# Second MLP of an attention-and-two-MLPs kernel: two weight-quadrant buffers, single transfers for a unit's weights, units split two ahead, four end buffers

## The chip, the cores and the metric

The kernel runs on one core of a Trainium2 chip. The metric is the time of one execution in microseconds of device time; where several executions are given, their median counts. All inputs and outputs are float32 in the core's HBM.

## The reference, cut to what matters

```python
def reference(**kwargs):
    attn_out = _attn_ref(...)              # windowed and global attention, 4 x 8 heads
    x = attn_out as (2304, 512)
    x = _moe_ref(x, w_gate, w_val, w_out, rms_g)   # first MLP, 512 -> 1536 -> 512
    return _moe2_ref(x, w_in, w_out)               # second MLP

def _moe2_ref(x, w_in, w_out):             # 2304 x 512, 512 x 2048, 2048 x 512
    h = x @ w_in
    g = np.maximum(0.01 * h, h)
    return (g @ w_out).astype(np.float32)
```

The change concerns the second MLP and the last stores of the first.

## The kernel before, in words

Every float32 matrix product is made of three passes: an operand is split into a high part (a cast on ScalarE, `high`) and a low part (a subtraction on VectorE, `low`), and `mm3` issues high x high, low x high and high x low. Attention and the first MLP run first, software-pipelined; at the end of each block of columns of the first MLP `out_half` copies the four accumulators `yp` to `ys` tiles (ScalarE and VectorE in turn, two buffers of tag `sq`) and stores them to `y_dram` in HBM. Meanwhile the weights of the second MLP are narrowed to float32 and stored to HBM as `w2_f32[f][0]` (first layer) and `w2_f32[f][1]` (second layer), f from 0 to 15. All of this is ordered by a planner that simulates the program.

The second MLP splits the 2,304 columns into a rest of 128 and two halves (s = 0, 1) of 1,024. For each half eight up steps (`up`, one for each pair j of weight chunks) and then eight down steps (`dn`) run. An up step makes the products of a 2 x 2 block scheme with seven products in place of eight (products 1, 6, 7, 5, 2, 4, 3, six matmuls of 512 columns each, in the banks px, pw, py, pz); VectorE adds the banks up (x1, u2, v, h), ScalarE applies the leaky function. A down step multiplies the hidden columns (split into `d`) with w_out and keeps eight accumulators `o`; the last down step of a half copies them to `ob` tiles, which use the places of x1, u2 and v, and stores them.

In the first half the weights of pair j are loaded as quadrants into the tile q (`load_q`, 512 KB in two transfers), summed on VectorE (`weight_sums`), split in two parts (`make_w` with place 0, 1 and 2, each called inside the up step of the pair before) and stored for the second half (`keep_parts`, 1.8 MB, transfer `w_dram<-wr`). The tile q has one buffer, and `load_q(j + 1)` follows `keep_parts(j)`. Pair 0 was prepared during the first MLP, and `load_q(1)` stands ahead of the hand-ordered part, where the planner places it.

The rest of 128 columns is computed in 32 small units, three matmuls each (bank pr in the first layer, po in the second), two to an up step: `rest_run` runs one at each of two places. A unit's 256 KB of weights are loaded by `rest_load` into one of two `raw` buffers (four transfers of 64 KB in the first layer), split by `rest_split` into an `rw` tile, and used by `rest_step`, which then splits the weights of the next unit and loads those of the third. `rest_first`, called in the first up step, loads the rest's 128 columns (transfer `yr<-y_dram`), splits them and unit 0. `rest_turn` transposes four hidden chunks (bank pt) into `hid`; every fourth unit of the second layer splits four of them into `hr`. Six `dop` buffers are shared by `rw` and `d`.

From the second MLP on, the order on TensorE, VectorE, ScalarE and SP is that of the program, written out by hand (`manual_schedule`); each engine runs its queue in order, and SP issues all the transfers. A tile of the second MLP's memory pool lies where tiles of the first MLP's pool lay, and its first use waits for those alone; tiles are laid out in the order of their first use.

Of the kernel before, what the change touches and what calls it, by code (L numbers as in the profile page):

```python
# [24 lines left out]
def tile_window_global_attention_two_mlps(  # L25
# [38 lines left out]
    w2_f32 = [[dram.tile([P, DM], F32, name=f"w2_f32{k}_{f}") for k in range(2)] for f in range(NF2)]  # L64
# [528 lines left out]
    def out_half(g, hs, m0):  # L593
        i, f = step_of(g)
        n = BLOCKS1[i]
        for m in range(m0, m0 + KC // 2):
            if f == 0:
                yp[i, m] = pools[0].tile([P, 512], F32, tag="y", bufs=4, name=f"yp{i}_{m}")
            mm3(yp[i, m][:, 0:n], [w[:, m * P:(m + 1) * P] for w in wsp[g, 2]], hs, f == 0, f == NF1 - 1)
        flush()  # L600
        if f == NF1 - 1:
            for m in range(m0, m0 + KC // 2):
                ys = mp.tile([P, NX], F32, tag="sq", bufs=2, name=f"ys{i}_{m}")
                if m % 2:
                    nc.vector.tensor_copy(ys[:, 0:n], yp[i, m][:, 0:n])
                else:
                    nc.scalar.copy(ys[:, 0:n], yp[i, m][:, 0:n])
                nc.sync.dma_start(out=y_dram[:, m, cols[i]:cols[i] + n], in_=ys[:, 0:n])
# [297 lines left out]
    def load_q(j):  # L906

        if j < PAIRS:
            q = wq[j] = quarter()
            for s, f in ((0, j + PAIRS), (2, j)):  # L910
                nc.sync.dma_start(out=q[:, s:s + 2].rearrange("p s c -> p (s c)"), in_=w2_f32[f][0])
# [16 lines left out]
    def make_w(g, place):  # L928
# [9 lines left out]
        elif s == 0:  # L938
# [5 lines left out]
            elif place == 1:  # L944
                low(wq["parts"][0][1], q[:, wq["parts"][0][2]], wq["parts"][0][0])
                high(wq["parts"][1][0], q[:, wq["parts"][1][2]])
            else:
                low(wq["parts"][1][1], q[:, wq["parts"][1][2]], wq["parts"][1][0])
                keep_parts(j)
                load_q(j + 1)  # L950
# [26 lines left out]
    def rest_load(u):  # L977
# [4 lines left out]
        if u < NRU:  # L982
            fq, kc = divmod(u, KC)
            for x in range(4):
                nc.sync.dma_start(out=raw[:, x * P:(x + 1) * P], in_=w2_f32[4 * fq + x][0][:, kc * P:(kc + 1) * P])
        else:
            nc.sync.dma_start(out=raw, in_=w2_f32[u - NRU][1])

    def rest_split(u):

        if u >= NRU + NF2:
            return
        t = rest["w", u] = halves_tile(f"rw{u}")
        split(t[:, 0], t[:, 1], rest.pop(("raw", u)))
        if u >= NRU and u % 4 == 0:
# [3 lines left out]
    def rest_first():  # L999
        y = wp2.tile([P, HALF], F32, tag="x1", name="yr32")  # L1000
        nc.sync.dma_start(out=y.rearrange("p (k c) -> p k c", k=KC), in_=y_dram[:, :, 0:REST])
        rest["y"] = wp2.tile([P, 2, KC, P], F32R, tag="yr", name="yr")
        split(rest["y"][:, 0].rearrange("p k c -> p (k c)"), rest["y"][:, 1].rearrange("p k c -> p (k c)"), y)
        rest["hid"] = wp2.tile([P, NF2, P], F32, tag="hid", name="hid")
        rest_split(0)
        rest_load(2)
# [7 lines left out]
    def rest_step(u):  # L1014
# [22 lines left out]
        if u + 1 != NRU:  # L1037
            rest_next(u)

    def rest_next(u):  # L1040
        rest_split(u + 1)
        rest_load(u + 3)

    units = [lambda u=u: rest_step(u) for u in range(NRU + NF2)]

    def rest_run(s, j, place):

        total = (s * PAIRS + j) * 2 + place + 1
        while units and NRU + NF2 - len(units) < total:
            units.pop(0)()  # L1050

    def hidden(s, j):
        return hid[s, j]
# [12 lines left out]
    def up(g):  # L1066
# [12 lines left out]
        if j == 0:  # L1079
            rest_first() if s == 0 else rest_next(NRU - 1)  # L1080
# [12 lines left out]
        make_w(g + 1, 2)  # L1093
        rest_run(s, j, 1)
# [12 lines left out]
    def dn(g):  # L1107
# [21 lines left out]
        else:  # L1129
            for x in (2, 3):  # L1130
                dop_of(s, 4 * j + x)
            make_w(g + 1, 0)
# [12 lines left out]
    load_q(1)  # L1145
    with tc.manual_schedule(engines={mybir.EngineType.PE, mybir.EngineType.DVE, mybir.EngineType.Activation,
                                     mybir.EngineType.SP}):
        rest_load(0)
# [62 lines left out]
```

## Time and profile before

| | us |
|---|---|
| three runs | 990.54, 992.22, 992.23 |
| median | 992.22 |
| the profiled execution | 993.27 |
| its span, first to last instruction | 991.5 |
| TensorE busy in the span | 938.8 (95%) |
| VectorE busy | 586.2 (59%) |
| ScalarE busy | 459.2 (46%) |
| mean granted TensorE clock | 0.981 |

All times in the views below are microseconds from the start of the span. In the rows PE is TensorE, PEld its weight loads, DVE is VectorE, ACT is ScalarE, SPq is the queue of transfers that SP issues. A line number belongs to the kernel before and can be that of a helper: L77 is `mm3`, L81 `high`, L84 `low`, L985 the unit's load in `rest_load`. Buffer numbers are left out of the names. A matmul's duration in a row overlaps with those of its neighbours, since matmuls are pipelined; the pace is read from the stretch, not from the mean of one. The granted clock is a share of 2.4 GHz, and the lower of the two levels is 1.2 GHz.

The second MLP begins near 599.5: first up stage to 717.05, first down stage to 805.71, second up stage to 900.32, second down stage to the end.

### The profile page before, as it was taken

The page shows a single profiled execution, that of the slowest core. Times are in us where ns is not written, and L with a number is a line of the kernel's source. Part 1 is how long each engine was busy: PE and PEld are TensorE (multiplying, and loading weights), DVE is VectorE, ACT ScalarE, POOL GpSimd, SP SyncE. Part 2 cuts the span into 40 slices and gives each one's busy share as a digit, 9 for nine tenths or more (in the row PEclk, how much of TensorE's full clock was granted, in tenths as well). Part 3 has the DMA queues.
Part 4 walks back from the last instruction along what each step waited for, and adds up shares of the span by engine and source line. Part 5 has one row for each costly group of instructions (what it writes and reads, how often), then busy time and mean ns, then how long its engine had stood idle before and what let it go on. Part 6 is the DMA issues. An engine that isn't in the chain of part 4 may idle for free.

```text
span 991.5 us, 14141 instructions
## 1 busy us (share of the span) xinstructions
PE 938.8 (95%) x5056; PEld 760.8 (77%) x5056; DVE 586.2 (59%) x1216; ACT 459.2 (46%) x958; POOL 4.5 (0%) x26
## 2 busy tenths in 40 slices
PE   6799989999999999999999997899899989999998
PEld 4557667777777777778999995676688768888886
DVE  5689975596576876535677634556535624445332
ACT  6877665565454654424544322334343423334322
POOL 1000000000000000000000000000000000000000
PEclk9899999999999999999999998999999989999999
DMA  9497994786769999544999942665522265551113
GB/s 314 151 308 258 298 321 153 259 307 213 265 225 368 348 369 365 175 145 147 339 298 318 377 141 80 223 221 204 172 81 86 64 244 198 195 211 55 43 43 106
DMA packets 87942, 215.38 MB, mean 217 GB/s; under 512 B 12224, under 2 KB 26048, under 8 KB 85824
## 3 DMA queue, kind: packets, MB, share of 16 engines
q1 hardware_dynamic: 87872, 214.47, 62.9%
q8 instruction: 40, 0.66, 0.3%
q14 instruction: 30, 0.25, 0.1%
HBM read 154.14 MB, written 60.29 MB: 216 GB/s over the span
## 4 chain that ended last, share of the span: by engine, by line
PE 61%; DMA 12%; DVE 7%; ACT 3%; SPq 3%; issue 2%; DVEq 0%; ACTq 0%
PE o L77 12%; PE pg L77 11%; PE yp L77 10%; PE pv L77 10%; PE pz L77 3%; PE py L77 2%; PE px L77 2%; DMA q<-y_dram 2%; PE po L145 2%; DMA wr<-w_f 2%; PE sc L145 2%; DMA raw<-w_f 2%; DMA w<-w 2%; DMA q<-w_f 2%; PE pp L254 1%
## 5 line engine op out<-in xcount | busy, mean ns | idle before, releaser
L77 PE MATMUL o<-wr,d 128*128 128x512 f32 x768 | 175.4, 390 | 0.6 <-DVE wr L84 0.5
L77 PEld LDWEIGHTS o<-wr,d 128*128 128x128 f32 x768 | 143.9, 188 | 31.8 <-DVE wr L84 1.0
L77 PE MATMUL pg<-xh,w 128*128 128x512 f32 (+1 forms) x464 | 132.6, 367 | 0.4 <-ACT xh L81 0.4
L77 PE MATMUL pv<-xh,w 128*128 128x512 f32 (+1 forms) x464 | 129.5, 361 | 0.0
L77 PE MATMUL yp<-hsh,w 128*128 128x512 f32 (+1 forms) x480 | 123.8, 365 | 2.3 <-ACT hsh L81 1.7
L77 PEld LDWEIGHTS yp<-hsh,w 128*128 128x128 f32 x480 | 83.6, 188 | 16.0 <-ACT hsh L81 2.8
L77 PEld LDWEIGHTS pg<-xh,w 128*128 128x128 f32 x464 | 80.8, 188 | 17.6 <-issue 5.6
L77 PEld LDWEIGHTS pv<-xh,w 128*128 128x128 f32 x464 | 82.3, 188 | 11.4 <-issue 0.9
L77 PE MATMUL pg<-xl,w 128*128 128x512 f32 (+1 forms) x232 | 83.2, 359 | 0.0
L77 PE MATMUL pv<-xl,w 128*128 128x512 f32 (+1 forms) x232 | 83.1, 358 | 0.0
L81 ACT CAST w<-wf 128x512 fp32r<-128x512 f32 x92 | 56.5, 615 | 43.1 <-PE yp L77 23.5
L77 PE MATMUL yp<-hsl,w 128*128 128x512 f32 (+1 forms) x240 | 74.9, 362 | 0.2 <-DVE hsl L84 0.2
L234 ACT ACTIVATE s_ring<-s_ring,mx 128x224 f32<-128x224 f32 x128 | 60.2, 472 | 31.0 <-DVE mx L231 30.7
L84 DVE TENSOR_TENSOR w<-wf,w 128x512 fp32r<-128x512 f32 x92 | 62.9, 685 | 16.2 <-ACT w L81 15.4
L77 PE MATMUL pz<-ysb,wr 128*128 128x512 f32 x192 | 56.3, 434 | 0.6
L84 DVE TENSOR_TENSOR wr<-wr 128x1024 fp32r<-128x1024 f32 x16 | 19.6, 1224 | 62.6 <-ACT wr L81 62.4
L81 ACT CAST hsh<-th 128x512 fp32r<-128x512 f32 (+1 forms) x60 | 33.3, 556 | 49.2 <-DVE th L826 48.1
L826 DVE SCALAR_TENSOR_TENSOR th<-th,pv 128x512 f32<-128x512 f32 (+1 forms) x60 | 36.2, 603 | 29.9 <-PE pv L77 29.3
L84 DVE TENSOR_TENSOR d<-h,d 128x512 fp32r<-128x512 f32 x64 | 41.1, 685 | 13.8 <-ACT d L81 13.6
L77 PEld LDWEIGHTS yp<-hsl,w 128*128 128x128 f32 x240 | 43.7, 188 | 6.6 <-DVE hsl L84 0.5
L77 PEld LDWEIGHTS pg<-xl,w 128*128 128x128 f32 x232 | 43.5, 188 | 6.7 <-DVE xl L84 0.3
L81 ACT CAST wr<-wr 128x1024 fp32r<-128x1024 f32 x16 | 16.8, 1050 | 67.4 <-DMA wr<-w_f 67.4
(158 smaller groups left out, 1480.0 us busy)
## 6 DMA issues: line engine op xcount, KB each, us to landing
w<-w_dram SPq DMA_DIRECT2D x84, 512.0 KB, 5.8
w<-w SPq DMA_DIRECT2D x36, 512.0 KB, 5.8
w_dram<-w SPq DMA_DIRECT2D x36, 512.0 KB, 4.1
w64b<-w SPq DMA_DIRECT2D x32, 512.0 KB, 6.8
wf<-w_f SPq DMA_DIRECT2D x60, 256.0 KB, 4.4
w_dram<-wr SPq DMA_DIRECT2D x8, 1792.0 KB, 6.8
wr<-w_dram SPq DMA_DIRECT2D x8, 1792.0 KB, 8.1
kq<-kqv SPq DMA_DIRECT2D x32, 352.0 KB, 5.2
```

What stands on the lines that cost most here:

```text
L77: nc.tensor.matmul(dst, lhs[a], rhs[b], start=first and i == 0, stop=last and i == 2, skip_group_check=onto)
L81: nc.scalar.copy(hi, src)
L84: nc.vector.tensor_tensor(out=lo, in0=src, in1=hi.bitcast(F32), op=ALU.subtract)
L145: x = nc.tensor.matmul(dst, lhs, rhs, start=start, stop=stop)
L234: x = nc.scalar.activation(out=sp, in_=sp, func=AF.Exp, bias=mx[:, c:c + 1], scale=-1.0, accum_out=sm[:, c:c + 1])
L254: nc.tensor.transpose(pp[:, n * P:(n + 1) * P], s[:, c0:c0 + P], ident)
L826: nc.vector.scalar_tensor_tensor(out=t, in0=t, scalar=0.5, in1=pp[1][:, 0:n], op0=ALU.mult, op1=ALU.mult)
```

## The change

Six things are changed:

- `load_q`: pairs with an even number are loaded into a tile of tag `h7` (the place of the last pair's hidden tile), those with an odd number into q as before; `load_q(j + 2)` follows `keep_parts(j)`. `load_q(1)`, `load_q(2)` and the load of the rest's columns now stand at the head of the hand-ordered part.
- The first-layer weights lie in four HBM tiles of four row blocks each (`w2_fours`), so that a unit's weights are one transfer of 256 KB.
- `rest_split` stands two units ahead of the use, and a split is followed by the load for the unit two further on.
- `BESIDE` gives the number of units in each up step: none in the first of the first half, then 3, 3, 2, 2, 2, 2, 2; two in each of the second half.
- `rest_first` is cut in three: the load at the start, the splits of the columns and of units 0 and 1 at the end of the first up step (`rest_second`), and the splits of the first hidden columns and of units 16 and 17 in the last down step of the first half (`rest_third`).
- At the end of the first MLP's last block the four `ys` tiles are the four parts of one tile (`ys_end`, tag `xh`) instead of two buffers in turn.

```diff
@@ -61,7 +61,8 @@
     y_dram = dram.tile([P, KC, NTOK], F32, name="y_dram")
     w1_f32 = [[dram.tile([P, DM], F32, name=f"w1_f32{k}_{f}") for k in range(3)] for f in range(NF1)]
     HK = KC // 2 * P
-    w2_f32 = [[dram.tile([P, DM], F32, name=f"w2_f32{k}_{f}") for k in range(2)] for f in range(NF2)]
+    w2_fours = [dram.tile([P, 4, DM], F32, name=f"w2_fours{f}") for f in range(NF2 // 4)]
+    w2_f32 = [(w2_fours[f // 4][:, f % 4], dram.tile([P, DM], F32, name=f"w2_f32_{f}")) for f in range(NF2)]
     w2_dram = [dram.tile([P, 2, 7 * HK], F32, name=f"w2_dram{j}") for j in range(NF2 // 2)]
     w1_dram = [[dram.tile([P, 2, DM], F32, name=f"w1_dram{k}_{f}") for k in range(3)] for f in range(NF1)]
     ph1 = ctx.enter_context(ExitStack())
@@ -599,8 +600,10 @@
             mm3(yp[i, m][:, 0:n], [w[:, m * P:(m + 1) * P] for w in wsp[g, 2]], hs, f == 0, f == NF1 - 1)
         flush()
         if f == NF1 - 1:
+            if i == NI - 1 and m0 == 0:
+                yp["end"] = mp.tile([P, KC, NX], F32, tag="xh", bufs=2, name="ys_end")
             for m in range(m0, m0 + KC // 2):
-                ys = mp.tile([P, NX], F32, tag="sq", bufs=2, name=f"ys{i}_{m}")
+                ys = yp["end"][:, m] if i == NI - 1 else mp.tile([P, NX], F32, tag="sq", bufs=2, name=f"ys{i}_{m}")
                 if m % 2:
                     nc.vector.tensor_copy(ys[:, 0:n], yp[i, m][:, 0:n])
                 else:
@@ -906,7 +909,7 @@
     def load_q(j):
 
         if j < PAIRS:
-            q = wq[j] = quarter()
+            q = wq[j] = quarter() if j % 2 else wp2.tile([P, 8, HK], F32, tag=f"h{PAIRS - 1}", name=f"q{j}")
             for s, f in ((0, j + PAIRS), (2, j)):
                 nc.sync.dma_start(out=q[:, s:s + 2].rearrange("p s c -> p (s c)"), in_=w2_f32[f][0])
 
@@ -947,7 +950,7 @@
             else:
                 low(wq["parts"][1][1], q[:, wq["parts"][1][2]], wq["parts"][1][0])
                 keep_parts(j)
-                load_q(j + 1)
+                load_q(j + 2)
 
 
     PRODUCT = {1: (1, "a", 0), 6: (4, "a", 1), 7: (5, "a", 2),
@@ -981,29 +984,38 @@
         raw = rest["raw", u] = wp2.tile([P, HALF], F32, tag="raw", bufs=2, name=f"raw{u}")
         if u < NRU:
             fq, kc = divmod(u, KC)
-            for x in range(4):
-                nc.sync.dma_start(out=raw[:, x * P:(x + 1) * P], in_=w2_f32[4 * fq + x][0][:, kc * P:(kc + 1) * P])
+            nc.sync.dma_start(out=raw.rearrange("p (f c) -> p f c", c=P), in_=w2_fours[fq][:, :, kc * P:(kc + 1) * P])
         else:
             nc.sync.dma_start(out=raw, in_=w2_f32[u - NRU][1])
 
     def rest_split(u):
 
-        if u >= NRU + NF2:
-            return
-        t = rest["w", u] = halves_tile(f"rw{u}")
-        split(t[:, 0], t[:, 1], rest.pop(("raw", u)))
-        if u >= NRU and u % 4 == 0:
+        if u < NRU + NF2:
+            t = rest["w", u] = halves_tile(f"rw{u}")
+            split(t[:, 0], t[:, 1], rest.pop(("raw", u)))
+            rest_load(u + 2)
+
+    def rest_cols(u):
+
+        if NRU <= u < NRU + NF2 and u % 4 == 0:
             t = rest["h"] = wp2.tile([P, 2, 4, P], F32R, tag="yr", name=f"hr{u}")
             split(t[:, 0], t[:, 1], rest["hid"][:, u - NRU:u - NRU + 4])
 
     def rest_first():
-        y = wp2.tile([P, HALF], F32, tag="x1", name="yr32")
-        nc.sync.dma_start(out=y.rearrange("p (k c) -> p k c", k=KC), in_=y_dram[:, :, 0:REST])
+        rest["y32"] = wp2.tile([P, HALF], F32, tag="hn", name="yr32")
+        nc.sync.dma_start(out=rest["y32"].rearrange("p (k c) -> p k c", k=KC), in_=y_dram[:, :, 0:REST])
+
+    def rest_second():
         rest["y"] = wp2.tile([P, 2, KC, P], F32R, tag="yr", name="yr")
-        split(rest["y"][:, 0].rearrange("p k c -> p (k c)"), rest["y"][:, 1].rearrange("p k c -> p (k c)"), y)
+        split(*(rest["y"][:, h].rearrange("p k c -> p (k c)") for h in range(2)), rest["y32"])
         rest["hid"] = wp2.tile([P, NF2, P], F32, tag="hid", name="hid")
         rest_split(0)
-        rest_load(2)
+        rest_split(1)
+
+    def rest_third():
+        rest_cols(NRU)
+        rest_split(NRU)
+        rest_split(NRU + 1)
 
     def rest_turn(fq, hn):
         pt = lone(f"pt{fq}")
@@ -1034,23 +1046,20 @@
                 store_rows(0, ob)
         if turn:
             rest_turn(*turn)
-        if u + 1 != NRU:
-            rest_next(u)
-
-    def rest_next(u):
-        rest_split(u + 1)
-        rest_load(u + 3)
+        if u < NRU - 2 or u >= NRU:
+            rest_cols(u + 1)
+            rest_split(u + 2)
 
     units = [lambda u=u: rest_step(u) for u in range(NRU + NF2)]
 
+
+    BESIDE = {0: (0, 3, 3, 2, 2, 2, 2, 2), 1: (2,) * 8}
+
     def rest_run(s, j, place):
 
-        total = (s * PAIRS + j) * 2 + place + 1
-        while units and NRU + NF2 - len(units) < total:
+        n = BESIDE[s][j]
+        for _ in range(n // 2 if place else n - n // 2):
             units.pop(0)()
-
-    def hidden(s, j):
-        return hid[s, j]
 
 
     SLOTS = ((0, 0), (0, 1), (1, 0), (1, 1))
@@ -1076,8 +1085,6 @@
         product(s, j, 7, by)
         plus(v, u2, by)
         make_w(g + 1, 0)
-        if j == 0:
-            rest_first() if s == 0 else rest_next(NRU - 1)
         rest_run(s, j, 0)
         bz = bank(f"pz{s}_{j}")
         product(s, j, 5, bz)
@@ -1091,6 +1098,8 @@
         product(s, j, 4, by, False)
         plus(h[:, 1], u2, by)
         make_w(g + 1, 2)
+        if (s, j) == (0, 0):
+            rest_second()
         rest_run(s, j, 1)
         product(s, j, 3, bz, False)
         plus(h[:, 2], u2, bz)
@@ -1129,6 +1138,8 @@
         else:
             for x in (2, 3):
                 dop_of(s, 4 * j + x)
+            if s == 0:
+                rest_third()
             make_w(g + 1, 0)
             for n, t in enumerate(range(NT2 - 1, -1, -1) if s else range(NT2)):
                 for x in range(4):
@@ -1142,9 +1153,11 @@
                 k, d = divmod(j - 1, 2)
                 dn.columns = (s + 1, k, d * HK, columns_in(s + 1, k, d * HK))
 
-    load_q(1)
     with tc.manual_schedule(engines={mybir.EngineType.PE, mybir.EngineType.DVE, mybir.EngineType.Activation,
                                      mybir.EngineType.SP}):
+        load_q(1)
+        load_q(2)
+        rest_first()
         rest_load(0)
         rest_load(1)
         for g in range(NU):
```

## Rows read from the trace of the kernel before

**Rows 1.** Busy time by stage: stretch, length, each engine, granted clock, DMA share, GB/s.
```profile
599.46:717.05 117.59, 101.29 (x398) 76.54 (x397) 62.25 (x101) 45.78 (x66) 0.00 (x0) 0.93 0.56 189
805.71:824.16 18.45, 14.37 (x53) 11.19 (x52) 6.86 (x11) 5.00 (x9) 0.00 (x0) 0.81 0.56 199
824.16:889.44 65.28, 65.28 (x289) 54.07 (x288) 29.89 (x45) 23.37 (x33) 0.00 (x0) 1.00 0.61 218
```

**Rows 2.** The same table for three weight pairs of the first up stage.
```profile
632.36:648.34 15.98, 13.43 (x54) 10.13 (x52) 9.19 (x15) 5.75 (x8) 0.00 (x0) 0.92 0.56 189
648.34:660.73 12.39, 12.13 (x49) 9.14 (x48) 6.72 (x13) 5.85 (x8) 0.00 (x0) 0.97 0.66 224
703.66:717.05 13.39, 11.79 (x49) 8.90 (x48) 5.24 (x8) 5.55 (x8) 0.00 (x0) 1.00 0.61 217
```

**Rows 3.** Waits, first up stage: who <- for whom: total us, times, longest.
```profile
ACT wr L81 <- DMA q<-w_f: 31.4, 6, 5.8
...
PE pr L77 <- ACT rw L81: 14.1, 8, 5.5
```

**Rows 4.** Timeline, fourth pair: start, duration, engine, operation, count, [idle before <-releaser].
```profile
633.44 0.32 SPq L681 DMA_DIRECT2D w_dram<-wr  x1
...
633.81 1.37 SPq L911 DMA_DIRECT2D q<-w_f  x2
...
642.43 0.83 ACT L81 CAST wr<-q 128x768 fp32r<-128x768 f32 x1 [5.82 <-DMA q<-w_f]
...
644.32 1.22 PE L77 MATMUL pr<-rw,yr 128*128 128x512 f32 x3 [2.46 <-ACT rw L81]
...
645.64 2.90 PE L77 MATMUL pz<-ysb,wr 128*128 128x512 f32 x6
```

**Rows 5.** Timeline, start of the second MLP.
```profile
599.67 3.21 SPq L608 DMA_DIRECT2D y_dram<-ys  x4
...
602.59 1.66 PE L77 MATMUL pw<-ysa,wr 128*128 128x512 f32 x6 [1.59 <-DVE ys L605]
602.93 3.80 SPq L985 DMA_DIRECT2D raw<-w_f  x8
...
604.49 0.84 ACT L81 CAST wr<-q 128x768 fp32r<-128x768 f32 x1 [2.00 <-DMA y_dram<-ys]
...
606.84 0.58 SPq L1001 DMA_DIRECT2D yr<-y_dram  x1
609.97 0.62 ACT L81 CAST yr<-yr 128x512 fp32r<-128x512 f32 x1 [4.64 <-DMA yr<-y_dram]
...
611.16 1.22 PE L77 MATMUL pr<-rw,yr 128*128 128x512 f32 x2 [5.55 <-ACT rw L81]
```

**Rows 6.** DMA issues, first up stage: transfer, count, KB each, median us to landing.
```profile
w_dram<-wr SPq DMA_DIRECT2D x7, 1792.0 KB, 6.8
raw<-w_f SPq DMA_DIRECT2D x64, 64.0 KB, 2.0
...
y_dram<-ys SPq DMA_DIRECT2D x4, 160.0 KB, 1.8
```

**Rows 7.** Landing of the two raw loads issued from 621.7 to 623.0.
```profile
DMA to landing us min/median/max: 5.6/6.1/6.6
```

**Rows 8.** Timeline of SP's queue, planned stretch: load of quadrants 1.
```profile
554.43 1.60 SPq L911 DMA_DIRECT2D q<-w_f  x2
```

**Rows 9.** Planned stretch 425 to 550: store of a narrowed weight, and busy time.
```profile
w_f<-wfb SPq DMA_DIRECT2D x6, 256.0 KB, 4.4
...
425.00:550.00 125.00, 123.16 (x771) 112.67 (x771) 78.50 (x151) 54.63 (x105) 0.00 (x0) 1.00 0.77 256
```

**Rows 10.** Timeline, turn from the first half to the second.
```profile
810.87 0.58 ACT L1073 COPY x<-px 128x512 f32<-128x512 f32 x1 [2.15 <-DMA out<-ob]
...
811.81 0.69 DVE L964 TENSOR_TENSOR u<-x,pw 128x512 f32<-128x512 f32 x1 [2.29 <-DMA out<-ob]
...
812.54 0.50 PE L77 MATMUL po<-rw,hr 128*128 128x512 f32 x1 [2.59 <-ACT hr L81]
```

## The prediction

> **What bounds the kernel now.** I read the stage table first [rows 1]. The first up stage of the second MLP (eight weight pairs on the first 1,024 columns, from the first px product to the first o product) lasts 117.59 us, with TensorE busy for 101.29 at a granted clock of 0.93. The second up stage does the same products: six of its pairs take 65.28 us, all busy at clock 1.00, so 10.88 us a pair of 48 matmuls, 0.2267 us each. The first up stage has 384 matmuls, 87.1 us at that pace, and twelve transposes of a quarter of the columns, some 0.7 (estimate from the same pace): floor 87.8, so 29.8 us are lost there. The turn between the halves (805.71 to 824.16) is one pair, floor 11.1 with four transposes, and takes 18.45 at clock 0.81: 7.3 lost.
>
> The pair windows [rows 2] alternate, 15.98 and 12.39 us. In neither is VectorE (9.19, 6.72) or ScalarE (5.75, 5.85) near its window. The waits [rows 3] tell who is last: TensorE waits 14.1 us for rw, which ScalarE makes, and ScalarE waits 31.4 us for the quadrant load q. The timeline shows the loop [rows 4]: at 633.44 SP issues the 1.8 MB store of finished weights, at 633.81 the load of the next quadrants into the only buffer, behind that store; ScalarE sits until 642.43 for it; the unit's split (rw) is queued behind it on ScalarE; so pr starts 2.46 us late at 644.32, and the next group of six matmuls takes 2.90 us, twice the 1.36 of full pace: the lower of the clock's two levels, 1.2 GHz (the window's mean is 0.92). The load can only be issued when the pair before has been split, so the loop is load (8.6 us) plus split and sums: longer than the 10.88 us of products.
>
> **Part by part.** *Two quadrant buffers, units split two ahead.* Quadrants j+2 are now loaded where j+1 were: landing 8.6 us after issue, needed about one and a half pairs (16 us) later. Hidden by 7 us; without that cover the cost is today's. A unit's split stands a pair earlier in ScalarE's queue, so a late load would no longer stop pr at once. What is late next is a chain through VectorE from one pair to the next: h2, leaky on ScalarE, x1, u2, v, four sums, rw low, h3, the last group of products. Five adds of 0.69 and x1 of 0.58 [rows 10], a group of 1.36, and some 3.5 for leaky and the sums (estimate, by their 1,536 and 1,024 columns against 512) are 8.9 us, under 10.88 but near it once each handover is added. DMA next: 189 GB/s over 117.59 us [rows 1] is 22.2 MB; in 94 us that is 236 GB/s. The plan's stretch of 425 to 550 moved 256 GB/s beside a TensorE that was busy for 123.16 of 125 us [rows 9]. So the stage ought to run at TensorE's pace, less the start.
>
> *The start.* Now [rows 5]: four copies through two buffers, the third and fourth waiting for stores; pw waits 1.59 us; then the first unit stops TensorE for 5.55 us, since its operands (yr) are loaded at 606.84, after eight issues for raw, and split only at 609.97. With four buffers each engine's second copy follows its first at once, and all end near 600.4 (estimate: half a microsecond a copy); pw has no wait, SP (0.32 us an issue [rows 4]) is through the four stores by 601.2. Unit 0 moves to pair 1, so the 5.55 us go, and the slow products after them. Against that, the load of quadrants 1, issued at 554.43 today [rows 8], moves behind the stores: the first manual issue today is raw at 602.93, straight behind the last store [rows 5], though its buffer had long been free. Issued at about 601.3 and 601.7, it lands after 1.8 (a store here [rows 6]) to 4.4 us (a 256 KB store [rows 9]); I take 3.1, the 256 KB yr load [rows 5], so 604.8 against 604.49 now: nothing, and 1 us at the far end. Behind it on ScalarE and VectorE stand the casts and sums, then h3, which the last products of pair 0 wait for. Tiles are laid out by first use: adding their sizes, v and wr now lie over the end buffers, so v waits for the last store: 601.2 + 1.8 = 603.0, before v is due at 603.6. No cost; 1 us if a store takes 2.5.
>
> So pair 0's 42 matmuls run through from 599.46 to 609.0. Pair 1 has three units, their splits two ahead, and raw 2 can be issued only when unit 0 is split (about 611.3), right behind the 1.8 MB store. Raw loads issued there land after 6.1 us [rows 7], so 617.5; with raw 3 beside it VectorE ends the split at 619.3. Unit 2 is due after 36 matmuls and two units, at 618.5: 0.8 us wait, then 0.7 for h3, which stands behind the splits on VectorE. In pair 2 the sixth raw load stands behind the next store in the same way: 1.2. These are 2.7 us. One of the stops may bring the lower clock as today's do: 1.4 us more, a group at 2.90 less 1.36 [rows 4]. Bounds: 0, if raw loads pass the store, to 9, if pairs 1 and 2 each lose what a slow pair loses today (15.98 - 11.5 [rows 2]). I take 4.1, nearest to the landing row.
>
> *One transfer in place of four.* Sixteen units save three issues each on SP; SP has slack, so nothing on the path. Bytes and 512-byte pieces are the same. The end of the stage (the w_out halves, whose load still stands behind the last weight store) I price at 0.8, one subtraction more ahead of the first o product; it is between 0 and today's 2.5 (13.39 less 10.88 [rows 2]).
>
> So the stage: 87.8 + 4.1 + 0.8 = 92.7, a gain of 24.9 us.
>
> *The turn.* Today ScalarE's copy x1 waits for an output store until 810.87, and behind it stand the splits of unit 16 and its hidden columns, so po starts 2.59 us late and slow [rows 10]. The change makes these splits in the last pair of the down stage, where three casts and three subtractions more meet an idle ScalarE and VectorE. Their cover: the products of 795 to 805. TensorE can then go from py to unit 16, the transposes and pz without x1. But raw 18 and 19 (512 KB) now stand ahead of the output stores on SP's queue: by (6.8 - 1.8) us for 1,792 KB [rows 6] that is 1.4 us later for the stores, so x1 starts at 812.3, u2 ends at 813.6 to 813.9, v at 814.6 (0.58 and 0.69 us each [rows 10]), then the fourth group, unit 17 and the last group end at 818.0. That is 12.3 instead of 18.45: gain 6.1. Bounds: 7.3, if the stores don't slip, to a loss of 1.4, if the splits gain nothing.
>
> Sum: 24.9 + 6.1 = 31.0. The profiled execution took 993.27 (span 991.5); 993.27 - 31.0 = 962.3. It lies 1.05 above the median of 992.22, so by that 961.2. The two down stages and the planned stretch I cost at nothing: their products are full already. For the plan, which is made anew, 2 us either way.
>
> **A rule weighed.** Raw loads issued behind the big store land after 6.1 us, where the median of all of them is 2.0 [rows 6, 7]. The Trainium skill (DMA: Bandwidth & Descriptors, "Queues, rings and completion order") says that one issuing engine's copies share its rings, and that each DMA engine consumes descriptors in ring order: a small load issued behind a large one waits. The trace agrees (6.1 against 2.0). By that rule a second quadrant buffer puts a further load ahead of the units' loads, which speaks against this change; it is the first rival. The same page's rules for authors ask to coalesce small transfers; four 64 KB loads in a row overlap here, so that saves issue time alone.
>
> **The rivals.** (1) *The units' loads become the bound.* If a raw load behind the store and two quadrant loads lands later than a pair after its issue, ScalarE stops at rw, and with it leaky, x1 and the next pair. For: 6.1 us already, while a load has some 9 us from issue to need. Against: today's better pairs take 12.39 us [rows 2] with the same loads one unit later. Price: every pair like those, 8 x 12.39 + 5 = 104; gain 13.4 + 6.1, time 972.7. (2) *The turn keeps its wait*, since output stores and x1 are later: 24.9 - 1.4, time 968.7. For: the stores' landing is the chain's step there. Against: pz needs none of them. (3) *The loads aren't early*: the second buffer is held by something else, the loop stays, and only the pw wait, the first unit's stop (some 4 us with its slow products) and the turn go: 12 us or less, 980 to 991, at the far end within 0.2%. For: h7's place has other uses. Against: h7 is written first in pair 7, two pairs after quadrants 6 are read. (4) *Slower*: the sixteen first-layer row blocks now lie interleaved in four HBM tiles. If writes to one tile are ordered among themselves, each store in the planned stretch waits on SP for the one before it, 4.4 us [rows 9], and weight loads queue behind. 16 x 4.4 = 70 us; from 1.9 us exposed per store the gain is gone, and with half exposed (35) the time is 996. For: SP does wait there for stores. Against: stores of one tile are far apart, and TensorE is full to 123.16 of 125 us.
>
> **How the numbers follow.** Forecast 0.68, rival 1 0.14, rival 2 0.08, rival 3 0.06 (0.02 of it within 0.2%), rival 4 0.04. Predicted: 961. The forecast's own range is 955 (both losses gone: 37.1) to 968 (the start at its far bound, plus the plan's 2). With rivals 1 and 2 the range is 955 to 975. Faster 0.94, same 0.02, slower 0.04; 0.2% is about what a measurement of this kernel can tell.
>
> **What would show it.** From first px to first o: 93 us at a clock of 0.97 or more; pairs 3 to 7 at 10.9 to 11.1. "ACT wr waits for DMA q" falls from 31.4 to under 4 us; what is left of TensorE's waits lies in pairs 1 and 2, behind raw. No wait at pw; first px product of pair 1 near 609. The turn: po for unit 16 within 1 us of py, 12 to 13 us in all, ended by x1's wait for the stores. Wrong, if pairs 3 to 7 stay above 12 us (rival 1), if q still ends ScalarE's waits (rival 3), if the turn stays above 17, or if the first px product of the stage is more than 2 us off 599.46 (rival 4).

## The result, and the profile after

The changed kernel takes 964.5 us (median of 961.7 to 967.4) where the kernel before takes 991.5 on the same chip: a ratio of 0.9729, with a 95% interval of 0.9696 to 0.9762. The profiled execution took 963.23 us, with a span of 961.5 against 991.5. The 30.0 us between the spans lie as follows. They are 3 us more than the 26.9 between the medians, since the profiled execution of the kernel before (993.27) was slower than its four runs (990.54 to 992.23) and that of the changed kernel faster than its median.

| stretch | before | after | gained |
|---|---|---|---|
| start to the first px product | 599.46 | 597.22 | 2.2 |
| first up stage | 117.59 | 95.36 | 22.2 |
| first down stage | 88.66 | 89.62 | -1.0 |
| turn | 18.45 | 11.83 | 6.6 |
| the rest | 167.34 | 167.47 | -0.1 |

The stage table of the changed kernel has the columns of [rows 1]. Its rows are the first up stage, its pairs 0 to 4 and 7, the first down stage and the turn.

```profile
597.22:692.58 95.36, 90.02 (x398) 72.76 (x396) 61.26 (x100) 46.20 (x65) 0.00 (x0) 1.00 0.71 234
597.22:606.77 9.55, 9.55 (x45) 7.89 (x43) 6.24 (x12) 4.72 (x9) 0.00 (x0) 1.00 0.71 206
606.77:621.74 14.97, 12.38 (x53) 9.41 (x52) 9.38 (x17) 5.88 (x8) 0.00 (x0) 1.00 0.68 219
621.74:635.59 13.85, 12.56 (x57) 9.81 (x55) 8.55 (x15) 7.58 (x11) 0.00 (x0) 1.00 0.70 235
635.59:646.47 10.88, 10.88 (x50) 9.01 (x48) 8.71 (x14) 5.35 (x7) 0.00 (x0) 1.00 0.83 270
646.47:657.84 11.37, 11.37 (x54) 9.40 (x53) 8.14 (x15) 6.70 (x9) 0.00 (x0) 1.00 0.76 256
...
680.08:692.58 12.50, 11.04 (x49) 8.82 (x47) 4.27 (x6) 4.06 (x6) 0.00 (x0) 1.00 0.62 219
692.58:782.20 89.62, 88.27 (x385) 71.95 (x386) 46.53 (x71) 35.59 (x53) 0.00 (x0) 1.00 0.31 99
782.20:794.03 11.83, 11.72 (x53) 9.13 (x51) 5.90 (x10) 3.87 (x7) 0.00 (x0) 1.00 0.79 291
```

Pairs 3 and 4 are full: 10.88 us, and 11.37 with four transposes, where the kernel before had 12.39 and 15.25. (The stretches of [rows 2] are its pairs 2, 3 and 7, counted from 0, and [rows 4] shows its pair 2.) What is still lost lies in pairs 1, 2 and 7. The waits of the stage say behind what:

```profile
ACT rw L82 <- DMA raw<-w_fours: 12.2, 7, 4.9
...
PE pz L78 <- DVE h L967: 2.2, 2, 1.3
...
PE pr L78 <- ACT rw L82: 1.7, 1, 1.7
```

The wait of [rows 3], ScalarE for the quadrant load (31.4 us), has no row any more. In its place ScalarE waits for raw, a unit's load, and TensorE's 14.1 us at pr are 1.7. The timeline of pair 1 shows that one stop and the one behind it:

```profile
609.34 10.82 SPq L987 DMA_DIRECT2D raw<-w_fours  x4
...
617.46 0.62 ACT L82 CAST rw<-raw 128x512 fp32r<-128x512 f32 x1 [4.89 <-DMA raw<-w_fours]
...
618.13 1.23 PE L78 MATMUL pr<-rw,yr 128*128 128x512 f32 x3 [1.68 <-ACT rw L82]
...
620.27 1.63 PE L78 MATMUL pz<-ysb,wr 128*128 128x512 f32 x6 [0.91 <-DVE h L967]
```

In the turn, ScalarE's x1 still waits for an output store, but TensorE is no longer behind it (compare [rows 10]):

```profile
786.27 0.84 PE L78 MATMUL po<-rw,hr 128*128 128x512 f32 x3
...
787.31 1.63 PE L78 MATMUL pz<-ysb,wr 128*128 128x512 f32 x6
787.87 0.59 ACT L1082 COPY x<-px 128x512 f32<-128x512 f32 x1 [2.18 <-DMA out<-ob]
```

py ends and po begins without a gap, pz runs ahead of x1, and the whole turn takes 11.83 us.

### The profile page after: what moved, and what is told of

It reads as the page before. It is cut to its first block, busy times and chain, and to the rows that moved or that the text cites. A ratio compares the mean times of both kernels' runs of the same rounds, so it can differ in the third digit from the quotient of the medians.

```text
span 961.5 us, 14038 instructions
## 1 busy us (share of the span) xinstructions
PE 925.0 (96%) x5056; PEld 755.1 (79%) x5056; DVE 585.5 (61%) x1216; ACT 461.0 (48%) x958; POOL 4.5 (0%) x26
## 4 chain that ended last, share of the span: by engine, by line
PE 71%; DMA 10%; DVE 4%; ACT 3%; issue 1%; SPq 1%; DVEq 0%; ACTq 0%
PE o L78 15%; PE pg L78 12%; PE yp L78 11%; PE pv L78 11%; PE px L78 3%; PE pz L78 3%; PE py L78 3%; PE po L146 2%; PE sc L146 2%; DMA raw<-w_fours 2%; PE pw L78 2%; DMA y_dram<-ys 2%; PE pp L255 2%; DMA q<-y_dram 2%; DMA wr<-w_f 2%
## 5 line engine op out<-in xcount | busy, mean ns | idle before, releaser
L78 PE MATMUL pz<-ysb,wr 128*128 128x512 f32 x192 | 49.4, 393 | 2.2 <-DVE h L967 2.2
```

Source lines behind the costliest of these rows:

```text
L78: nc.tensor.matmul(dst, lhs[a], rhs[b], start=first and i == 0, stop=last and i == 2, skip_group_check=onto)
```

## The experiments

Each was timed in four runs beside the kernel before. The changed kernel itself, run again with the first experiments as their yardstick, took 963.4 us: 0.9734 of before (0.9719 to 0.9749). Its profile, the second of this program, has 94.73 us for the first up stage, 91.19 for the first down stage and 12.77 for the turn; the stages below are compared with these.

> The changed kernel again, for comparison on one chip with what follows and for a second profile. Expected 962 to 967 us; first up stage 95 to 96 us with the two stops in pairs 1 and 2 (about 3.4 and 2 us), turn 11.8 us. If the first px product starts 2 us away from 597.2, the gain of 2.2 us ahead of the second MLP is no part of the change.

The first px product starts at 594.85, so the 2.2 us are no part of the change. The turn misses what was expected by 1 us: x1 begins 6.46 us after the turn's first product, where it was 5.67 in the first profile.

### Which part opens the loop

**One quadrant buffer in the changed kernel.**

```diff
-            q = wq[j] = quarter() if j % 2 else wp2.tile([P, 8, HK], F32, tag=f"h{PAIRS - 1}", name=f"q{j}")
+            q = wq[j] = quarter()
...
-                load_q(j + 2)
+                load_q(j + 1)
...
-        load_q(2)
```

> The changed kernel with one quadrant buffer, loaded where it was loaded before (j + 1 behind the store of j); all else as changed. Theory (the single buffer's loop of load, sums and splits is longer than a pair's products): load 8 us and about 6 us from landing to the next store, so 14 to 15 us a pair, first up stage 110 to 115 us, time 979 to 985 us. Rival (what stopped TensorE was the units' splits standing behind the load on ScalarE, and these now stand a pair earlier): stage below 100 us, time below 970 us.

980.0 us, 0.9895 of before (0.9877 to 0.9913). The first up stage takes 113.14 us instead of 94.73, while the turn (12.29) keeps its gain. Three rows of its waits in that stage:

```profile
ACT wr L82 <- DMA q<-w_fours: 25.7, 5, 5.6
...
PE pz L78 <- DVE h L967: 9.0, 5, 2.8
...
PE pt L1023 <- ACT hn L970: 5.6, 1, 5.6
```

The windows of pair 4 and of the stage:

```profile
654.39:668.90 14.51, 11.66 (x54) 9.33 (x52) 7.99 (x14) 5.75 (x8) 0.00 (x0) 1.00 0.59 199
597.46:710.60 113.14, 95.38 (x398) 75.78 (x396) 61.89 (x100) 45.13 (x65) 0.00 (x0) 0.95 0.59 199
```

The quadrant wait is back, and the pairs with it. But TensorE stops at the last group, pz, whose sum h3 stands behind the late splits on VectorE, and no longer at pr: a unit split two ahead is ready before the late load stops ScalarE. The longest single stop, 5.6 us, is at the transposes of pair 2, whose input hn ScalarE makes behind that load; pair 2 takes 20.62 us. So the look-ahead moves the stop from pr to what comes next behind the load, and doesn't remove it.

**Two quadrant buffers alone, in the kernel before.**

```diff
-            q = wq[j] = quarter()
+            q = wq[j] = quarter() if j % 2 else wp2.tile([P, 8, HK], F32, tag=f"h{PAIRS - 1}", name=f"q{j}")
...
-                load_q(j + 1)
+                load_q(j + 2)
...
+        load_q(2)
         rest_load(0)
```

> The kernel before with two quadrant buffers and nothing else changed: load of quadrants j + 2 behind the store of j, the load of quadrants 2 at the head of the hand-ordered part. Theory: the loop goes, pairs 2 to 7 at 10.9 to 11.6 us; the wait at pw, the stop of 5.6 us at the first unit and the turn of 18.5 us stay: 974 to 979 us. Rival: units stay behind late loads and the time stays within 4 us of 991.

974.0 us, 0.9838 (0.9823 to 0.9852). Windows of pairs 0, 1, 2 and 7:

```profile
593.55:615.95 22.40, 14.18 (x51) 10.67 (x49) 8.99 (x16) 5.65 (x10) 0.00 (x0) 0.77 0.36 111
615.95:626.83 10.88, 10.88 (x50) 9.01 (x48) 7.91 (x14) 5.97 (x8) 0.00 (x0) 1.00 0.79 265
626.83:638.20 11.37, 11.37 (x54) 9.40 (x53) 8.08 (x14) 6.03 (x8) 0.00 (x0) 1.00 0.76 256
...
682.69:697.94 15.25, 12.60 (x50) 9.79 (x48) 6.18 (x10) 5.64 (x8) 0.00 (x0) 0.89 0.55 190
```

The second buffer by itself fills pairs 1 to 6, with units split one ahead and four small loads each. What it leaves is the first pair (22.40, with the waits at pw and at the first unit), the last pair, and the turn (18.42). These are what the other parts are for, and this kernel is 10.5 us behind the full change (963.4), run beside it.

**Units split one ahead, the rest as changed.**

```diff
-        if u < NRU - 2 or u >= NRU:
-            rest_cols(u + 1)
-            rest_split(u + 2)
+        if u + 1 != NRU:
+            rest_cols(u + 1)
+            rest_split(u + 1)
```

(`rest_second` and `rest_third` then split one unit instead of two.)

> The changed kernel with the units split one ahead as before, two quadrant buffers kept. Theory: the quadrant loads were the bound, so 964 to 969 us, at most 4 us more, from raw loads that now stop TensorE sooner in pairs 1 to 7. Rival (the units' look-ahead made the gain): the stops at pr come back in every pair, 12.4 us a pair or more, time above 974 us.

964.0 us, 0.9743 (0.9726 to 0.9759): the same as the change. Its windows show why, pairs 1 and 7 and the first down stage:

```profile
603.63:619.82 16.19, 13.75 (x53) 10.55 (x52) 9.88 (x17) 5.88 (x8) 0.00 (x0) 0.89 0.59 194
678.34:694.45 16.11, 13.06 (x50) 9.87 (x48) 6.64 (x10) 5.64 (x8) 0.00 (x0) 0.90 0.50 180
694.45:782.77 88.32, 87.79 (x386) 71.91 (x384) 44.66 (x67) 33.96 (x51) 0.00 (x0) 1.00 0.31 99
```

In the up stage the look-ahead is worth 5.6 us (100.37 against 94.73), in pairs 1 and 7 alone. But here the last pair, late by its last unit, leaves the w_out halves time to arrive: no stop at the first o product, and the down stage takes 88.32 instead of 91.19 (89.62 in the first profile). So the second unit of look-ahead gained nothing in this kernel's time. Whether it pays once that next stop is gone, no run here shows.

### The start

**Two end buffers again.**

```diff
-            if i == NI - 1 and m0 == 0:
-                yp["end"] = mp.tile([P, KC, NX], F32, tag="xh", bufs=2, name="ys_end")
...
-                ys = yp["end"][:, m] if i == NI - 1 else mp.tile([P, NX], F32, tag="sq", bufs=2, name=f"ys{i}_{m}")
+                ys = mp.tile([P, NX], F32, tag="sq", bufs=2, name=f"ys{i}_{m}")
```

> The changed kernel with the two end buffers of before. Theory: the third and fourth copies wait for stores again, pw waits about 1.6 us, and quadrants 2, the rest's columns and raw are issued about 1.5 us later: pair 0 at 11 to 12 us instead of 9.55, the other pairs as changed, time 1.5 to 3 us above the changed kernel (964.5 to 967). Rival (pair 0's start hides the copies): pair 0 stays below 10 us.

965.6 us, 0.9744 (0.9709 to 0.9779). Pair 0 takes 11.42 us instead of 9.55, and the timeline has the reason:

```profile
600.17 1.64 PE L78 MATMUL pw<-ysa,wr 128*128 128x512 f32 x6 [1.58 <-DVE ys L606]
```

It is the wait of [rows 5] (1.59) again. The four end buffers are worth these 1.9 us; the total can't resolve them.

**Units from pair 0 on, two in each pair.**

```diff
-    BESIDE = {0: (0, 3, 3, 2, 2, 2, 2, 2), 1: (2,) * 8}
+    BESIDE = {0: (2, 2, 2, 2, 2, 2, 2, 2), 1: (2,) * 8}
...
         make_w(g + 1, 0)
+        if (s, j) == (0, 0):
+            rest_second()
         rest_run(s, j, 0)
```

(`rest_second` is taken out of its place at the end of the step.)

> The changed kernel with units from the first pair on, as before (two in each pair, the splits of the rest's columns and of units 0 and 1 ahead of them in pair 0). The loads stay at the head. Theory (pair 0 has no time for them: columns and weights are issued behind the stores near 600 and land 4 to 5 us later, and ScalarE and VectorE are busy with the casts and sums of quadrants 1): TensorE stops 3 to 6 us at pr in pair 0, pair 0 at 14 to 16 us, but pairs 1 and 2 have two units and lose less, 11 to 13 us each; time 963 to 968 us. Rival (only the early loads matter): pair 0 below 12 us and the time below the changed kernel's.

964.4 us, 0.9735 (0.9714 to 0.9755). Pair 0 takes 18.40 us, more than the 14 to 16 expected; the chain to its stop at the first unit:

```profile
602.37 0.62 ACT L82 CAST yr<-yr 128x512 fp32r<-128x512 f32 x1 [3.20 <-DMA yr<-y_dram]
...
603.91 1.65 PE L78 MATMUL pr<-rw,yr 128*128 128x512 f32 x3 [4.92 <-ACT rw L82]
```

But with two units each pairs 1 and 2 are full, and the stage (97.32) is only 2.6 us longer than the yardstick's. An empty first pair gains 8.9 us there (18.40 less 9.55), and the third units of pairs 1 and 2 give most of it back.

**Three raw buffers, loaded three units ahead.**

```diff
-        raw = rest["raw", u] = wp2.tile([P, HALF], F32, tag="raw", bufs=2, name=f"raw{u}")
+        raw = rest["raw", u] = wp2.tile([P, HALF], F32, tag="raw", bufs=3, name=f"raw{u}")
...
-            rest_load(u + 2)
+            rest_load(u + 3)
```

(One more load at the head.)

> The changed kernel with three raw buffers, each unit's load issued three units ahead. Theory for what is still lost in pairs 1 and 2 (raw loads issued behind the 1.8 MB weight store, 8 us to landing): unit 2's weights are there, so the stop at pr in pair 1 (1.2 to 1.7 us) goes, but unit 3's split stands at the same place and still waits on ScalarE: pair 1 at 13 to 14 us instead of 14.5 to 15, pair 2 at 12 to 13, time 960 to 963. Rival (the three units of pairs 1 and 2 overload VectorE): pairs 1 and 2 stay at 14.5 and 13.9.

959.4 us, 0.9692 (0.9666 to 0.9717). The stop at pr in pair 1 is gone, but the stage is no shorter (94.54). The windows of pairs 1 and 2:

```profile
604.36:618.23 13.87, 11.93 (x52) 9.50 (x51) 9.39 (x17) 6.51 (x10) 0.00 (x0) 0.99 0.77 244
618.23:632.07 13.84, 13.83 (x57) 11.04 (x55) 9.60 (x16) 6.96 (x10) 0.00 (x0) 0.88 0.70 233
```

Pair 1 ends with a stop of 1.94 us at pz, behind VectorE's h, which stands behind the split of the next unit; ScalarE waits 4.00 us for that unit's load. Pair 2 then has no stop at all, but runs at clock 0.88. So I was wrong about pair 2: its loss here is the slower clock, not a load. The 4 us in the total lie in the down stage and the turn, 88.61 and 11.61 against 91.19 and 12.77, not in the stage at which the edit was aimed. Against the first profile of the changed kernel (89.62 and 11.83) these two give 1.2 us; what the edit does there wasn't tested.

**Three raw buffers, and the third units moved to pairs 6 and 7.** The edit of the three raw buffers, and

```diff
-    BESIDE = {0: (0, 3, 3, 2, 2, 2, 2, 2), 1: (2,) * 8}
+    BESIDE = {0: (0, 2, 2, 2, 2, 2, 3, 3), 1: (2,) * 8}
```

> As the one with three raw buffers, and two units a pair from pair 1 on, three in pairs 6 and 7. Theory (late raw loads): each load now has 9 us or more from issue to need, pairs 1 and 2 come down to 10.9 to 11.4 us, the first up stage to 90 to 92 us, time 957 to 961. Rival (VectorE overloaded by three units): pairs 1 and 2 are fast and pairs 6 and 7 lose the same instead, time as the changed kernel's.

956.6 us, 0.9668 (0.9633 to 0.9703). Pairs 1 to 5 are full (10.88 to 11.37), and the stage takes 91.21. The last unit stops TensorE for 1.73 us at pr in pair 7, since its split stands behind the cast of the late w_out half on ScalarE:

```profile
680.47 1.04 ACT L82 CAST wr<-wr 128x1024 fp32r<-128x1024 f32 x1 [6.58 <-issue]
681.42 0.61 ACT L82 CAST rw<-raw 128x512 fp32r<-128x512 f32 x1
...
682.08 1.22 PE L78 MATMUL pr<-rw,yr 128*128 128x512 f32 x3 [1.73 <-ACT rw L82]
```

### The end of the stage and the turn

**The last weight store behind the loads of w_out.**

```diff
-                keep_parts(j)
+                if j < PAIRS - 1:
+                    keep_parts(j)
...
         fetch_w(g + 1)
+        if (s, j) == (0, PAIRS - 1):
+            keep_parts(j)
```

> The changed kernel with the last weight store of the first up stage (pair 7) issued behind the loads of the first w_out halves, not ahead of them. Theory (these loads are late behind 1.8 MB and stop TensorE at the first o product): pair 7 at 10.9 to 11.3 us instead of 12.4, no stop at o, the down stage at 88.3 instead of 89.6 to 91.2; time 960 to 962. Rival (the loads are held by the buffer that the products of pair 6 free): pair 7 stays above 12 us.

959.9 us, 0.9693 (0.9652 to 0.9734). SP's queue at the end of the stage:

```profile
680.55 0.84 SPq L926 DMA_DIRECT2D wr<-w_f  x2
681.44 0.42 SPq L684 DMA_DIRECT2D w_dram<-wr  x1
```

The window of pair 7:

```profile
679.50:690.38 10.88, 10.88 (x49) 9.01 (x48) 6.28 (x9) 5.23 (x7) 0.00 (x0) 1.00 0.62 242
```

The last pair is full and the down stage starts without a stop. It takes 89.28 us, not the 88.3 expected: two later waits for weights, 0.9 and 0.5 us, stand near its end.

**The splits of the turn back in the turn.**

```diff
         make_w(g + 1, 0)
+        if (s, j) == (1, 0):
+            rest_third()
...
-            if s == 0:
-                rest_third()
```

> The changed kernel with the splits of the first hidden columns and of units 16 and 17 put back into the first up step of the second half. Theory (they stood behind x1 on ScalarE, and x1 behind an output store): TensorE waits 2 to 3 us at po again and runs slow after it, turn 17 to 19 us, time 968 to 972 us. Rival (the turn's gain came from the weights' earlier state elsewhere): turn stays near 12 us.

967.0 us, 0.9772 (0.9742 to 0.9801), 1 us under what was expected. The turn takes 19.01 us:

```profile
785.39 0.59 ACT L1082 COPY x<-px 128x512 f32<-128x512 f32 x1 [2.14 <-DMA out<-ob]
787.07 0.79 PE L78 MATMUL po<-rw,hr 128*128 128x512 f32 x1 [4.15 <-ACT rw L82]
```

po waits behind x1 as in [rows 10]. The whole gain of the turn is this move, and the total, 3.5 us up on the yardstick, falls short of the 6.2 by which the turns differ; this kernel's down stage was 1.9 shorter (89.29 against 91.19).

### The transfers

**Four transfers of 64 KB for a unit again.**

```diff
-            nc.sync.dma_start(out=raw.rearrange("p (f c) -> p f c", c=P), in_=w2_fours[fq][:, :, kc * P:(kc + 1) * P])
+            for x in range(4):
+                nc.sync.dma_start(out=raw[:, x * P:(x + 1) * P], in_=w2_f32[4 * fq + x][0][:, kc * P:(kc + 1) * P])
```

> The changed kernel with each first-layer unit's weights in four transfers of 64 KB again. Theory (issue time of SP alone, off the path): time within 2 us of the changed kernel, the same stage length within 1 us. Rival (four completions behind the store land later than one): pairs 1 and 2 lose 1 us each more.

962.8 us, 0.9731 (0.9700 to 0.9762): no difference. A small piece lands earlier (median of the first up stage 3.2 us against 5.0), but a split needs the fourth. The four pieces of the unit that pair 1 waits for, behind the weight store:

```profile
L988 SPq DMA_DIRECT2D raw<-w_fours x4: 491/848/1303, 615.0 to 618.1; - x4
...
DMA to landing us min/median/max: 4.8/5.6/7.2
```

The first piece has the longest time and the last the shortest. The last, issued at 618.1, lands at 622.9, 7.9 us after the first was issued; in the changed kernel this unit took 8.1 as one transfer. Pairs 1 and 2 took 15.6 and 13.27, against 14.97 and 13.85. Pair 7 took 10.89, without a stop at its end.

### A version that beats both

**Three raw buffers, third units in pairs 5 and 6, the last store behind w_out.** The edits of the three raw buffers and of the last store, and

```diff
-    BESIDE = {0: (0, 3, 3, 2, 2, 2, 2, 2), 1: (2,) * 8}
+    BESIDE = {0: (0, 2, 2, 2, 2, 3, 3, 2), 1: (2,) * 8}
```

> Three raw buffers, two units a pair from pair 1 on and three in pairs 5 and 6, and the last weight store behind the w_out loads. Theory: all three remaining losses of the first up stage go together: pairs 1 to 7 at 10.9 to 12.0 us, no stop of TensorE above 0.5 us from the first px product to the first o product, stage 88 to 89 us, time 952 to 955 us. Rival (three units late in the stage overload VectorE): pairs 5 and 6 lose 1 us or more beyond their 11.6 and 11.9, time 956 or more.

956.1 us, 0.9659 of before (0.9629 to 0.9690). The windows of pairs 1 and 6 and of the whole stage:

```profile
606.10:616.98 10.88, 10.88 (x49) 9.01 (x48) 8.71 (x16) 5.69 (x8) 0.00 (x0) 1.00 0.88 281
...
662.15:674.41 12.26, 12.25 (x56) 9.89 (x55) 8.59 (x15) 6.96 (x10) 0.00 (x0) 1.00 0.63 214
...
596.55:685.29 88.74, 88.73 (x398) 73.18 (x397) 63.19 (x103) 46.96 (x66) 0.00 (x0) 1.00 0.76 253
```

TensorE is busy for 88.73 of the stage's 88.74 us, and the products and transposes at full pace are 88.5 (384 times 0.2267 and three times 0.49). So hardly anything is left to win in this stage but the products themselves. The time expected was 952 to 955; the median missed that by 1 us, with the stage where it was put.

## Why the prediction was right, step by step

The time (961 predicted, 964.5 measured) and the mechanism hold. Of the sum, 24.9 for the first up stage and 6.1 for the turn, 22.2 and 6.6 came. That the profiled execution (963.23) lies within 1 us of the 962.3 forecast for it is in part luck: 2.2 us of its gain lie ahead of the second MLP and can't be credited to the change.

**The loop: right.** The second buffer alone fills pairs 1 to 6 of the old kernel, and taking it out of the new one brings the quadrant wait back. The chain through VectorE, put at 8.9 us a pair, stays under 10.88: pairs with two units have no stop. DMA has the room that I worked out: 234 GB/s over the stage (236 predicted), and up to 281 in a pair of the last version.

**Two units ahead: right about pr, but for nothing yet.** The split one ahead costs 5.6 us of the stage, all in pairs 1 and 7, and nothing in the total.

**The start: right about pair 0 (9.55 for 9.54), wrong about the load of quadrants 1.** I let it move behind the end stores, arguing from raw's issue at 602.93. SP's queue shows that it didn't move:

```profile
551.64 1.54 SPq L914 DMA_DIRECT2D q<-w_fours  x2
...
597.43 1.79 SPq L611 DMA_DIRECT2D y_dram<-ys_end  x4
599.27 0.95 SPq L914 DMA_DIRECT2D q<-w_fours  x2
```

Quadrants 1 are still issued early, as in [rows 8], although the call now stands in the hand-ordered part; only quadrants 2 follow the stores. Why raw waited for the stores and this load doesn't isn't tested here. The sum had this step at nothing, so no number fell with it.

**The mis-sized term: unit loads behind the big store.** I charged pairs 1 and 2 with 2.7 us of waits and 1.4 of slower clock, 4.1 in all. Three units in a pair are 51 products, 11.56 us, and a set of transposes 0.49 (11.37 less 10.88). So pair 1 lost 14.97 - 11.56 = 3.4 and pair 2 lost 13.85 - 12.05 = 1.8: together 5.2, at a clock of 1.00, so it is 3.9 us of waits (1.68, 0.91, and 1.28 at pz in pair 2) and the restarts after them, and the slower clock that I charged didn't come. (A full pair with three units and transposes took 12.04 in pair 5 of the last version.) The step that was off is the landing time of 6.1 us from [rows 7]. These are not two loads, as I read them, but the first two of the four 64 KB pieces of one load. All four, in the kernel before:

```profile
L985 SPq DMA_DIRECT2D raw<-w_f x4: 476/853/1267, 621.7 to 624.8; - x4
...
DMA to landing us min/median/max: 4.2/5.1/6.6
```

The fourth, issued at 624.8 and landing after 4.2, completes the unit 7.3 us after its first issue. In the changed kernel a whole unit is one transfer. The two loads issued at 609.3 and 610.7:

```profile
DMA to landing us min/median/max: 7.6/7.8/8.1
```

The load that stops pr is the first of them, with 8.1: 2.0 us more than the 6.1 in the sum. Reading half a unit makes 1.2 of these. The other 0.8 isn't the size of the transfer, since in four pieces the unit takes 7.9 in the changed kernel too; its cause stays open. A row used for a term has to hold everything that is waited for. The stop at pr grew by only 0.9 (1.68 for 0.8), because a second error pulled the other way: pr starts 0.67 us after ScalarE begins the cast rw, and I had let it wait for VectorE's subtraction too.

The Trainium skill's rule on ring order (DMA: Bandwidth & Descriptors, "Queues, rings and completion order"), which I took for a rival only, agrees with this landing: 7.6 to 8.1 us behind the weight store, against 3.3 for the unit load issued at 618.8. That wait was the larger cost in the two pairs with three units. In pairs with two, where the load has longer until it is needed, it cost nothing.

**The end: too small.** 0.8 was charged; pair 7 lost 12.50 - 10.88 = 1.6. TensorE stops at the first o product, behind ScalarE's cast of w_out and then of d. The second w_out load was issued at 682.3, behind the last weight store:

```profile
DMA to landing us min/median/max: 8.1/8.1/8.1
```

With the store behind the loads it took 3.6, and the pair is full. But the store ahead doesn't always cost this: in the kernel with four small transfers it stands ahead too, the same load took 6.5, and the pair (10.89) is full as well. Why it landed earlier there stays open. Transposes were put at 0.7 for the stage and are three times 0.49, 0.8 more. Together: 1.1 (pairs 1 and 2), 0.8 (pair 7) and 0.8 (transposes) make the 2.7 between 92.7 and 95.36.

**The turn: right; its slip of 1.4 us isn't shown.** 11.83 us, and 12.77 in the second profile, against 12.3. x1 begins 5.67 us after the turn's first product (6.46 in the second profile), where it was 810.87 - 805.71 = 5.16. I put a slip of 1.4 down to raw 18 and 19 ahead of the output stores, and the runs don't bear that out. The first output store is issued 8.71 us ahead of the turn in both kernels. With one or both of these loads ahead of it x1 came at 5.04 to 6.71 us over eleven profiles; with them behind it at 5.16, 5.63 and 6.84 (the kernel before, the one with two quadrant buffers alone, and the one with the splits moved back). With the splits moved back, the turn is 19.01: the cause of the gain is shown.

**One transfer in place of four: nothing, as said.** The Trainium skill asks to coalesce small transfers (DMA: Bandwidth & Descriptors, "Rules for kernel authors"); here 64 transfers of 64 KB and 16 of 256 KB take the same time, 962.8 and 963.4 us: in this kernel it gained nothing at that size.

**The planned stretch: nothing can be read from it.** My test for rival 4 was a first px product within 2 us of 599.46. It came 2.2 us early, and in a second profile of the same program 4.6 early (594.85). Over all these kernels it lies from 593.55 to 602.94, and the earliest is the old kernel with two buffers, whose weights lie in the old HBM tiles. As far as these runs show, the spread belongs to the executions and not to the tiles: the test was too fine, and the 2.2 us in the table can't be credited to the change.

**The rivals.** Rival 1 (every pair at 12.39) is refuted by pairs 3 to 6, although its mechanism is what pairs 1 and 2 lost by. Rival 2 is refuted by the turn, rival 3 by the missing quadrant wait. Rival 4, slower by 1.9 us or more exposed per store, would at the half exposed that I priced have put the first px product 35 us late, and it came early.

## What to carry to other kernels

Where the loop of load, split and compute was longer than its products, a second buffer for the one load that is issued last ended it; look-ahead on the other operands only moved the stop to the next thing queued behind that load. After that, count what stands ahead of each load on its queue: a third buffer for the units' weights, third units where the loads have time, and a store behind the loads that are needed sooner took a further 7 us. Price a load behind a large store by the time at which its last piece lands, not by that of its first pieces.

## What the runs showed of the hardware that was not expected

Stops of much the same length didn't have the same effect on TensorE's clock. In the changed kernel the first o product comes after a stop of 1.46 us, and the clock stays at 1.00. In the second profile of the same program the stop there was 1.29, and the next 8 us ran at 0.79. The timeline of the changed kernel:

```profile
692.58 0.50 PE L78 MATMUL o<-wr,d 128*128 128x512 f32 x1 [1.46 <-ACT d L82]
```

The timeline of the second profile:

```profile
689.58 0.49 PE L78 MATMUL o<-wr,d 128*128 128x512 f32 x1 [1.29 <-ACT d L82]
```

Its window from there on:

```profile
689.58:697.58 8.00, 7.63 (x25) 5.94 (x26) 5.84 (x10) 5.99 (x9) 0.00 (x0) 0.79 0.17 60
```

That is most of what sets its down stage at 91.19 against 89.62. With three raw buffers a stop of 1.94 us was followed by a pair at 0.88, while 1.68 and 0.91 us in pair 1 of the changed kernel left 1.00. The length of the stop doesn't decide it: at the first o product stops of 2.24 us (one quadrant buffer) and 1.76 (three raw buffers) left the next 8 us at 1.00, and one of 1.16 (two end buffers) was followed by 0.79. So a small stop can carry some 1.6 to 1.8 us behind it that its own row doesn't show (91.19 less 89.62; 13.84 less the 12.05 of a full pair 2). What decides it stayed open.
